# An mLSTM cell feeding a SwiGLU block: the first group's own results in two halves of 64 tokens, and a new order of the prologue

## The chip, the cores and the metric

The kernel runs on one core of a Trainium2 chip. The metric is the device time in microseconds, the median over several executions. One more execution is taken by the hardware profiler. The engines are TensorE (PE; PEld is its weight load), VectorE (DVE), ScalarE (ACT), GpSimd (POOL) and SyncE (SP), which only issues transfers.

## The reference

Two parts follow one another. The first is an mLSTM cell over 4 batches of 8 heads, 768 tokens and head size 40, a recurrence with stabilised gates:

```
m_new  = max(f + m, i);  f_stab = exp(f + m - m_new);  i_stab = exp(i - m_new)
C      = f_stab * C + i_stab * outer(v, k);   n = f_stab * n + i_stab * k
y      = sigmoid(o) * (C @ q) / max(|n . q|, 1)
```

The result, 3072 tokens of 320 features, goes through a SwiGLU block with 1536 hidden features: `(silu(x @ w_gate) * (x @ w_val)) @ w_out`. The weights come as 64-bit floating-point numbers, so that the kernel has to convert them; everything else is float32.

## The kernel before, in words

**Tiling.** The 768 tokens of each of the 4 batches are cut into 6 groups of 128 tokens. A group of all four batches has 512 rows, which is the width of a matmul in the SwiGLU block. While TensorE does the SwiGLU block of one group (12 hidden blocks of 128 features, `hidden`, L643, then the projection), the cell of the next group is computed in between. Nothing can run ahead of the first group's cell, so the kernel has a prologue of its own for it, and that is what the change rewrites.

**The prologue.** The recurrence is computed in parallel form within the group: weights of decay between every pair of tokens (`W0`, exponentials of gate sums, zero where the key comes after the query), multiplied by the scores q.k (`first_scores`, L513), multiplied by the values (`first_own`, L527). The values carry a column of ones, so that the product also gives the denominator. A unit `u` is one batch, that is 8 heads; a half `P` is two batches. `first_turn` (L503) transposes keys and queries by TensorE, `first_x` (L532) divides by the denominator, `first_gate` (L541) multiplies by the sigmoid of the output gates (`sig`, L462), `first_seam` (L558) transposes the result into the layout that the SwiGLU block reads, and `first_state` (L547) makes the state that the next group starts from, which `first_kept` (L555) copies out of PSUM. `first_values` (L499) prepares the values for that state on GpSimd. `burn` (L466) is dummy matmuls that keep TensorE from standing idle.

**The weights.** A piece of the 64-bit weights is asked for by `piece_load` (L140): the gate half goes into partitions 0 to 63 on SP's queue and the value half into partitions 64 to 127 on ScalarE's queue. A block of it is converted in three steps: `scale` (L185; ScalarE scales the upper and then the lower 32-bit words), `join` (L195; two VectorE operations shift and mask the upper part) and `rounded` (L204; an integer addition of the lower part, on VectorE where the call says V, else on GpSimd). The first hidden block needs block 0, the second block 1, and so on. Pieces 2 and 3 land in memory that the hidden results will use later; piece 2's is also part of `W0`, so that it is asked for only when the third own product has been made.

**Order.** There is no scheduler: each engine and each queue runs its instructions in the order of the program's calls and waits only on semaphores. An instruction that waits holds up all that stands behind it on its engine, the transfers that the engine issues among them. PSUM is given out in two rings of four banks, "cell" and "gen". `late_sums` (L273; a scan on VectorE, then a clearing and a subtraction on GpSimd) belongs to the gates of the later groups and is needed by `late_maxima`, which runs behind the first hidden block.

Of the kernel before, what the change touches and what calls it, by code (L numbers as in the profile page):

```python
# [19 lines left out]
SUB = 64  # L20
# [4 lines left out]
def kernel(  # L25
# [50 lines left out]
    def bank(name, tag="cell"):  # L76
        return psum.tile([128, 512], F32, name=name, tag=tag)
# [41 lines left out]
    def copy(eng, dst, src):  # L119
        if eng is nc.scalar:  # L120
            nc.scalar.copy(dst, src)
        else:
            eng.tensor_copy(dst, src)
# [58 lines left out]
                for c in range(0, n, 2):  # L182
                    blocks[NFC + (m + c) // 2] = (lo[:, c:c + 2], hi[:, c:c + 2], wo_sb[:, m + c:m + c + 2, :])

    def scale(j):  # L185
        if j in blocks:
            lo, hi, dst = blocks[j]
            a, d = hi.shape[1], hi.shape[2]
            top = conv.tile([128, NKC * 128], F32, name="top", bufs=1).rearrange("p (a d) -> p a d", a=a)
            nc.scalar.mul(top, hi.bitcast(F32), 2.0 ** -112)  # L190
            low = conv.tile([128, NKC * 128], I32, name="low").rearrange("p (a d) -> p a d", a=a)
            nc.scalar.mul(low, lo, 2.0 ** -29)
            blocks[j] = (low, top.bitcast(U32), dst)

    def join(j):  # L195
        if j in blocks:
# [76 lines left out]
    def late_sums():  # L273
        nc.vector.tensor_tensor_scan(flat(f_sb), flat(keep1), flat(f_sb), 0.0, op0=ALU.mult, op1=ALU.add)
        nc.gpsimd.memset(step1, 0.0)
        nc.gpsimd.tensor_sub(i_sb, i_sb, f_sb)
# [11 lines left out]
    M_dram = tc.dram_tile([BH, S - L], F32, name="M_dram")  # L288


    def turn_one(P, src, dst, engs):
        tp = [bank("tp_kq").rearrange("p (a t) -> p a t", t=SUB) for _ in range(2)]
        for a in range(UA):
            h = P * UH + 2 * a
            for i in range(2):
                nc.tensor.transpose(tp[i][:, a, :], src[half(i), h:h + 2, :].rearrange("p h d -> p (h d)"),  # L296
                                    ident[half(i), half(i)])
        for i in range(2):
            copy(engs[i], dst[:, P * UA:(P + 1) * UA, half(i)], tp[i])
# [128 lines left out]
    def xT(n):  # L428
        return xTs[max(n - 1, 0) % 2]
# [32 lines left out]
    def sig(P):  # L462
        nc.scalar.activation(o_sb[:, heads(P)], o_sb[:, heads(P)], AF.Sigmoid)
# [8 lines left out]
        return slice(u * BH, (u + 1) * BH)  # L472

    A, V, G = nc.scalar, nc.vector, nc.gpsimd
    HH = H // 2
    wps = {}

# [26 lines left out]
    def first_turn(P, src, dst, engs):  # L504
        for b in range(2):
            tp = bank("tp_kq").rearrange("p (a t) -> p a t", t=L)
            for a in range(UA // 2):
                h = P * UH + b * H + 2 * a
                nc.tensor.transpose(tp[:, a, :], src[:, h:h + 2, :].rearrange("p h d -> p (h d)"), ident)  # L509
            a = P * UA + b * UA // 2  # L510
            copy(engs[b], dst[:, a:a + UA // 2, :], tp)
# [15 lines left out]
    def first_own(u):  # L527
        first_y[u] = bank("first_y", "gen")[:, 0:H * D1].rearrange("p (h d) -> p h d", d=D1)
        for h in range(H):
            nc.tensor.matmul(first_y[u][:, h, :], lhsT=W0[:, u * H + h, :], rhs=v_sb[:, u * H + h, :], start=True, stop=True)  # L530

    def first_x(u):  # L532
        y = first_y.pop(u)
# [4 lines left out]
        nc.vector.tensor_tensor(x_sb[:, u, 0:DM].rearrange("p (h d) -> p h d", d=D), y[:, :, 0:D],  # L538
                                den.to_broadcast([128, H, D]), op=ALU.mult)

    def first_gate(P):  # L541
        for u in (2 * P, 2 * P + 1):
            x = x_sb[:, u, 0:DM].rearrange("p (h d) -> p h d", d=D)
            nc.vector.tensor_tensor(x, x, o_sb[:, u * H:(u + 1) * H], op=ALU.mult)
# [10 lines left out]
    def first_kept(P, ps, eng):  # L555
        copy(eng, state(2)[:, P * UA:(P + 1) * UA], ps)

    def first_seam(P, engs):  # L558
# [53 lines left out]
    nc.scalar.activation(warm, warm, AF.Silu)  # L612
    piece_load(4, wo_sb)
    piece_load(5)
# [106 lines left out]
        for P in range(2):  # L721
            load(dst, a, n, P)

    run = lambda f, *a, **b: (lambda: f(*a, **b))


    on_vector = (9, 10, 11)
# [125 lines left out]
```

## Time and profile before

| what | value |
|---|---|
| runs before | 552.24, 552.34, 552.70 us; median 552.34 |
| profiled execution | 551.99 us, its span 550.0 us |
| TensorE busy | 544.9 us (99%), granted clock 1.00 |
| VectorE, ScalarE, GpSimd busy | 236.1, 136.1, 103.0 us |
| first matmul of the SwiGLU block | 32.04 us from the start of the span |
| busy from 15.00 to 32.04 us | TensorE 16.69, VectorE 14.08, ScalarE 8.20, GpSimd 4.15 us |
| second output gates | asked for at 16.83 us, landed 8.2 us later |
| first weights, gate half | asked for at 19.43 us, landed 8.8 us later |

Times in the profile count from the start of the span. Busy time of an engine is the union of its instructions; matmuls are pipelined, so a busy TensorE is not one at its peak. A row of the timeline merges consecutive instructions of one line and gives the idle time ahead of them and what ended it. A float32 matmul leaves two records, [...]; a transpose leaves one. The chain that ended last is followed back from the last instruction to whatever released it.

### The profile page before, as it was taken

The page shows a single profiled execution, that of the slowest core. Times are in us where ns is not written, and L with a number is a line of the kernel's source. Part 1 is how long each engine was busy: PE and PEld are TensorE (multiplying, and loading weights), DVE is VectorE, ACT ScalarE, POOL GpSimd, SP SyncE. Part 2 cuts the span into 40 slices and gives each one's busy share as a digit, 9 for nine tenths or more (in the row PEclk, how much of TensorE's full clock was granted, in tenths as well). Part 3 has the DMA queues.
Part 4 walks back from the last instruction along what each step waited for, and adds up shares of the span by engine and source line. Part 5 has one row for each costly group of instructions (what it writes and reads, how often), then busy time and mean ns, then how long its engine had stood idle before and what let it go on. Part 6 is the DMA issues. An engine that isn't in the chain of part 4 may idle for free.

```text
span 550.0 us, 11592 instructions
## 1 busy us (share of the span) xinstructions
PE 544.9 (99%) x4989; PEld 311.4 (57%) x4989; DVE 236.1 (43%) x397; ACT 136.1 (25%) x203; POOL 103.0 (19%) x95
## 2 busy tenths in 40 slices
PE   8999999999999999999999999999999999999997
PEld 4964556774555575545575545576455567444475
DVE  5778668961346232455421545531436621111100
ACT  4376755352110133011024101115110100111100
POOL 2304265673011060011133011124001100000000
PEclk9999999999999999999999999999999999999999
DMA  9999997878431762660564551395000131000000
GB/s 123 177 294 184 188 277 154 146 104 118 53 49 23 120 112 64 74 74 11 87 117 104 63 72 14 59 146 113 1 1 2 32 63 40 12 1 0 2 24 24
DMA packets 223994, 45.69 MB, mean 83 GB/s; under 512 B 214504, under 2 KB 219112, under 8 KB 223944
## 3 DMA queue, kind: packets, MB, share of 16 engines
q1 hardware_dynamic: 222036, 42.11, 46.7%
q10 hardware_dynamic: 1908, 2.85, 1.9%
q8 instruction: 39, 0.64, 0.5%
q14 instruction: 11, 0.09, 0.1%
HBM read 35.68 MB, written 4.01 MB: 72 GB/s over the span
## 4 chain that ended last, share of the span: by engine, by line
PE 98%; DVE 1%; ACT 0%; issue 0%; ACTq 0%; DVEq 0%
PE gv_ps L651 57%; PE o_ps L667 24%; PE o_ps L674 5%; PE inter L377 2%; PE sp L331 2%; PE intra L382 2%; PE add L353 1%; PE first_y L530 1%; PE burn L469 1%; PE tp_kq L509 1%; PE sp L519 1%; PE wps L480 0%; PE tp_kq L296 0%; PE wps L484 0%; PE wps L489 0%; PE tp_x L439 0%
## 5 line engine op out<-in xcount | busy, mean ns | idle before, releaser
L651 PE MATMUL gv_ps<-xT,wgv_sb 64*128 64x512 f32 x1440 | 316.6, 593 | 0.3 <-DVE wgv_sb L207 0.3
L651 PEld LDWEIGHTS gv_ps<-xT,wgv_sb 64*128 64x128 f32 x1440 | 138.1, 187 | 159.1 <-issue 156.4
L657 DVE TENSOR_TENSOR h_sb<-sg,gv_ps 128x512 f32<-128x512 f32 x72 | 49.5, 688 | 212.3 <-ACT sg L656 212.3
L667 PE MATMUL o_ps<-wo_sb,h_sb 128*128 128x320 f32 x480 | 130.5, 433 | 0.0
L667 PEld LDWEIGHTS o_ps<-wo_sb,h_sb 128*128 128x128 f32 x480 | 90.8, 190 | 41.0 <-issue 3.8
L656 ACT ACTIVATE sg<-gv_ps 128x512 f32<-128x512 f32 x72 | 43.0, 597 | 263.7 <-PE gv_ps L651 263.7
L456 POOL TENSOR_SCALAR_AFFINE_SELECT w_sb<-w_sb 64x1024 f32<-64x1024 f32 x20 | 28.5, 1423 | 63.9 <-DVE w_sb L451 62.9
L362 POOL TENSOR_TENSOR C<-C,dec 128x328 f32<-128x328 f32 x20 | 14.5, 738 | 134.8 <-DVE C L369 134.8
L661 ACT COPY z_sb<-o_ps 128x320 f32<-128x320 f32 x24 | 10.0, 423 | 93.2 <-PE o_ps L667 89.4
L403 POOL TENSOR_TENSOR o_sb<-o_sb,y_sb 128x640 f32<-128x640 f32 x10 | 14.2, 1431 | 78.9 <-DVE y_sb L394 78.9
L674 PE MATMUL o_ps<-wo_sb,h_sb 128*128 128x320 f32 x96 | 26.9, 437 | 0.0
L451 DVE TENSOR_TENSOR w_sb<-g_T,w_sb 128x1024 f32<-128x1024 f32 x10 | 13.1, 1354 | 28.6 <-DMA w_sb<-M_dram 28.6
L426 DVE STREAM_TRANSPOSE xT<-x_sq 128x640 f32<-128x640 f32 x16 | 12.5, 822 | 22.9 <-DMA x_sq<-x_sb 22.9
L674 PEld LDWEIGHTS o_ps<-wo_sb,h_sb 128*128 128x128 f32 x96 | 17.9, 190 | 7.2
L394 DVE TENSOR_TENSOR y_sb<-y_sb,intra 64x328 f32<-64x328 f32 x40 | 19.7, 492 | 0.7
L369 DVE TENSOR_TENSOR C<-C,add 40x328 f32<-40x328 f32 (+1 forms) x36 | 17.7, 493 | 1.2 <-POOL C L362 0.6
L377 PEld LDWEIGHTS inter<-C,qT 64*64 64x64 f32 x640 | 10.2, 134 | 7.3 <-issue 6.1
L460 ACT ACTIVATE w_sb<-w_sb 128x1024 f32<-128x1024 f32 x10 | 10.6, 1058 | 12.7 <-POOL w_sb L456 12.7
L207 POOL TENSOR_TENSOR wgv_sb<-wgv_sb,low 128x640 int32<-128x640 int32 x6 | 9.3, 1546 | 23.5 <-DVE wgv_sb L200 23.5
L341 POOL TENSOR_TENSOR vw_sb<-v_sb,w_sb 128x656 f32<-128x656 f32 x10 | 12.8, 1306 | 0.4
L338 DVE TENSOR_TENSOR w_sb<-sp,w_sb 128x512 f32<-128x512 f32 x20 | 12.7, 682 | 0.0
L397 DVE TENSOR_SCALAR den<-den 128x16 f32<-128x16 f32 x10 | 12.2, 1215 | 0.3
(132 smaller groups left out, 344.5 us busy)
## 6 DMA issues: line engine op xcount, KB each, us to landing
w_sb<-M_dram SPq DMA_DIRECT2D x10, 512.0 KB, 7.3
x_sq<-x_sb SPq DMA_DIRECT2D x128, 40.0 KB, 2.0
k_sb<-in_k_dram SPq DMA_DIRECT2D x12, 320.0 KB, 6.0
v_sb<-in_v_dram SPq DMA_DIRECT2D x12, 320.0 KB, 5.6
o_sb<-in_o_gate_dram SPq DMA_DIRECT2D x12, 320.0 KB, 5.5
raw<-in_moe_w_out_dram SPq DMA_DIRECT2D x3, 1280.0 KB, 7.5
out_dram<-z_sb SPq DMA_DIRECT2D x24, 160.0 KB, 1.8
q_sb<-in_q_dram SPq DMA_DIRECT2D x32, 64.0 KB, 2.3
```

The costliest lines, as they stand in the source:

```text
L362: nc.gpsimd.tensor_tensor(state(s + 1)[:, a], state(s)[:, a], dec[:, s - 2, a].unsqueeze(2).to_broadcast([128, UA, D1]), op=ALU.mult)
L369: nc.vector.tensor_tensor(c, c, ps[r], op=ALU.add)
L377: nc.tensor.matmul(inter[two][half(i), a, :], lhsT=qT[half(two), P * UA + a, half(i)], rhs=state(2 * n + i)[half(two), P * UA + a, :], sta ...
L394: nc.vector.tensor_tensor(t, t, intra[i][half(c)], op=ALU.add)
L403: eng.tensor_tensor(o, o, y[:, :, 0:D], op=ALU.mult)
L451: nc.vector.tensor_tensor(w_sb[:, heads(P)], gb, w_sb[:, heads(P)], op=ALU.subtract)
L456: nc.gpsimd.affine_select(w, w, compare_op=ALU.is_ge, fill=NEG, base=0, pattern=[[0, UH], [1, SUB]], channel_multiplier=-1)
L651: nc.tensor.matmul(ps[i], lhsT=wgv_sb[half(i), m, PAIRS[kc][i] if g < 2 else kc, :], rhs=x[half(i), kc, :], start=(kc == 0), stop=(kc == N ...
L656: nc.scalar.activation(sg, ps[0], AF.Silu)
L657: nc.vector.tensor_tensor(hid(g, m), sg, ps[1], op=ALU.mult)
L667: nc.tensor.matmul(p, lhsT=hid(g, m)[:, ts(u, L)], rhs=wo_sb[:, m, :], start=(m == 0), stop=(m == NFC - 1))
L674: nc.tensor.matmul(ps[u], lhsT=hid(g, m)[:, ts(u, L)], rhs=wo_sb[:, m, :], start=(m == 0), stop=(m == NFC - 1))
```

## The change

Five things are changed, all ahead of the first hidden block or beside it.

1. The own product of a unit is made in two halves. Queries 64 to 127 take all 128 keys, queries 0 to 63 only the first 64 keys, and the two land in different partitions of one bank.
2. The keys and queries of the second half of the batches are transposed by `turn_one`, the form of the later groups, which works on 64 tokens at a time and takes two banks.
3. The order is new: the second own product comes between the transposes of the second half's keys and those of its queries, no longer behind both, the first state ahead of the first seam, and the calls of `burn` are others (7 more at the start in both; 6 before, 14 after).
4. The first piece of weights is asked for ahead of the second output gates, and the second piece directly behind them, ahead of the first `sig`. `scale` is split in two, so that the upper words of block 0 are scaled, and the block joined, ahead of the second `sig` and the second gating. The second gating, the second `sig` and the lower words come behind the first copy of the first seam. The first gating is made by GpSimd.
5. `late_sums` moves from behind the first own product to behind the conversion of block 1. Both state copies are ScalarE's.

```diff
-    def scale(j):
+    def scale_top(j):
...
+    def scale_low(j):
...
+    def scale(j):
+        scale_top(j)
+        scale_low(j)
...
-            nc.tensor.matmul(first_y[u][:, h, :], lhsT=W0[:, u * H + h, :], rhs=v_sb[:, u * H + h, :], start=True, stop=True)
+            n = u * H + h
+            nc.tensor.matmul(first_y[u][half(1), h, :], lhsT=W0[:, n, half(1)], rhs=v_sb[:, n, :], start=True, stop=True)
+            nc.tensor.matmul(first_y[u][half(0), h, :], lhsT=W0[half(0), n, half(0)], rhs=v_sb[half(0), n, :], start=True,
+                             stop=True)
...
-            nc.vector.tensor_tensor(x, x, o_sb[:, u * H:(u + 1) * H], op=ALU.mult)
+            eng.tensor_tensor(x, x, o_sb[:, u * H:(u + 1) * H], op=ALU.mult)
...
             copy(eng, xT(0)[:, c:c + len(cs), 2 * P * L:(2 * P + 2) * L].rearrange("p c (u s) -> p c u s", u=2), tp)
+            for f in between.get(c, ()):
+                f()
...
     first_own(0)
-    late_sums()
-    first_turn(1, k_sb, kT, (A, A))
+    turn_one(1, k_sb, kT, (A, A), "gen")
+    first_own(1)
+    turn_one(1, q_sb, qT, (A, V))
     first_x(0)
-    first_turn(1, q_sb, qT, (A, V))
+    piece_load(0)
     load(o_sb, o_gate, 0, 1)
-    piece_load(0)
-    first_own(1)
+    piece_load(1)
     first_values(1)
+    burn(3)
     first_scores(1)
     first_x(1)
     sig(0)
-    piece_load(1)
-    burn(3)
+    burn(2)
     first_own(2)
     piece_load(2, h_sb[:, 1:1 + NKC])
-    sig(1)
     burn(2)
     first_own(3)
-    first_gate(0)
+    ps0 = first_state(0, "gen")
+    burn(2)
+    first_gate(0, G)
     first_x(2)
     first_x(3)
-    first_gate(1)
-    first_seam(0, (A, A, V))
-    scale(0)
+    scale_top(0)
+    join(0)
+    first_seam(0, (A, A, V), {0: [run(sig, 1), run(first_gate, 1, V), run(scale_low, 0)]})
     ps1 = first_state(1, "gen")
-    burn(1, "gen")
+    burn(5)
     piece_load(3, h_sb[:, NH - NKC:])
-    join(0)
+    rounded(0, V)
     first_seam(1, (A, A, V))
-    rounded(0, V)
-    first_kept(0, first_state(0), A)
-    first_kept(1, ps1, V)
+    first_kept(0, ps0, A)
+    first_kept(1, ps1, A)
     convert(1, V)
+    late_sums()
     nc.scalar.activation(warm, warm, AF.Silu)
```

More of the change, by code (lines that the diff above doesn't have):

```diff
@@ L190, in scale @@
             nc.scalar.mul(top, hi.bitcast(F32), 2.0 ** -112)
+            blocks[j] = (lo, top.bitcast(U32), dst)
+    def scale_low(j):
+        if j in blocks:
+            lo, *rest = blocks[j]
+            a, d = lo.shape[1], lo.shape[2]
             low = conv.tile([128, NKC * 128], I32, name="low").rearrange("p (a d) -> p a d", a=a)
             nc.scalar.mul(low, lo, 2.0 ** -29)
-            blocks[j] = (low, top.bitcast(U32), dst)
+            blocks[j] = (low, *rest)
+    def scale(j):
+        scale_top(j)
+        scale_low(j)
     def join(j):
@@ L288, with turn_one @@
     M_dram = tc.dram_tile([BH, S - L], F32, name="M_dram")
-    def turn_one(P, src, dst, engs):
-        tp = [bank("tp_kq").rearrange("p (a t) -> p a t", t=SUB) for _ in range(2)]
+    def turn_one(P, src, dst, engs, tag="cell"):
+        tp = [bank("tp_kq", tag).rearrange("p (a t) -> p a t", t=SUB) for _ in range(2)]
         for a in range(UA):
@@ L474 @@
     A, V, G = nc.scalar, nc.vector, nc.gpsimd
+    run = lambda f, *a, **b: (lambda: f(*a, **b))
     HH = H // 2
@@ L539, in first_x, with first_gate @@
                                 den.to_broadcast([128, H, D]), op=ALU.mult)
-    def first_gate(P):
+    def first_gate(P, eng):
         for u in (2 * P, 2 * P + 1):
             x = x_sb[:, u, 0:DM].rearrange("p (h d) -> p h d", d=D)
-            nc.vector.tensor_tensor(x, x, o_sb[:, u * H:(u + 1) * H], op=ALU.mult)
+            eng.tensor_tensor(x, x, o_sb[:, u * H:(u + 1) * H], op=ALU.mult)
         nc.gpsimd.tensor_copy(x_sb[:, 2 * P:2 * P + 2, DM:], x_sb[:, 2 * P:2 * P + 2, 0:HP])
@@ L556, in first_kept, with first_seam @@
         copy(eng, state(2)[:, P * UA:(P + 1) * UA], ps)
-    def first_seam(P, engs):
+    def first_seam(P, engs, between={}):
         for c, eng in zip(range(0, NKC, 2), engs):
@@ L722, in load_all @@
             load(dst, a, n, P)
-    run = lambda f, *a, **b: (lambda: f(*a, **b))
     on_vector = (9, 10, 11)
```

## The prediction

> **What bounds it now.** I read the engines' busy shares first: TensorE is busy 544.9 of 550.0 us. The waits of TensorE then name the only places where it stands still after its first 1.2 us, 0.7 us in all.
>
> ```profile
> PE gv_ps L651 <- DVE wgv_sb L207: 0.3, 1, 0.3
> PE sp L519 <- ACT qT L121: 0.2, 1, 0.2
> PE first_y L530 <- DVE h_sb L523: 0.2, 1, 0.2
> ```
>
> So everything after the first gate/value matmul (32.04 us) is TensorE without a gap. The change touches only what lies before it and the three blocks after it: its worth is the shift of that start, call it G, plus any stall that it makes behind G. The chain that ended last shows what sets G (start, length, what):
>
> ```profile
> 25.39 1.73 PE first_y L530 x16
> 27.78 0.49 DVE x_sb L538
> 28.27 0.80 DVE x_sb L544 x2
> 29.43 0.50 DVE wgv_sb L199
> 29.95 0.83 DVE wgv_sb L200
> 31.08 0.83 DVE wgv_sb L207
> 32.04 17.51 PE gv_ps L651 x80
> ```
>
> TensorE's last own product releases DVE, and DVE goes through dividing, gating and joining the first weights. The timeline of TensorE shows that it was itself busy until 31.76 us, so G has two bounds 0.3 us apart: a gain must shorten both. Rows with the prices I need (start, length, engine, line, shapes, count):
>
> ```profile
> 18.63 1.88 PE L530 MATMUL first_y<-v_sb,h_sb 128*128 128x41 f32 x16
> 28.15 1.13 PE L552 MATMUL add<-vw_sb,k_sb 128*64 128x41 f32 x32
> 17.73 1.06 PE L509 MATMUL tp_kq<-ident,q_sb 128*128 128x128 f32 x8
> 59.57 0.66 PE L296 MATMUL tp_kq<-ident,k_sb 64*128 64x64 f32 x16
> 25.72 0.74 ACT L463 ACTIVATE o_sb<-o_sb 128x640 f32<-128x640 f32 x1 [3.61 <-DMA raw<-in_moe_w_val_dram]
> 16.10 1.47 DVE L274 TENSOR_TENSOR_SCAN f_sb<-keep,f_sb 32x640 f32<-32x640 f32 x1
> 58.53 1.14 DVE L199 TENSOR_SCALAR wgv_sb<-top 128x640 uint32<-128x640 uint32 x1 [0.91 <-ACT top L190]
> 57.77 1.55 POOL L207 TENSOR_TENSOR wgv_sb<-wgv_sb,low 128x640 int32<-128x640 int32 x1 [2.55 <-DVE wgv_sb L200]
> ```
>
> [...] the shift at 58.53 takes 1.14 us under GpSimd's addition, which ends at 59.32, and 0.49 us elsewhere. [...] the first 128*64 product's weights load at 28.151, 0.20 us after the last transpose began, where 0.11 is normal; after a 41-column product a change takes 0.155 us instead of 0.05 or less. No run here alternates two shapes on disjoint parts of the array. [...] for the small weights: 198 GB/s at 26 to 30 us.
>
> **The change, part by part.**
> TensorE. An own product of 16 records (1.71 us start to next) becomes 16 products in two column halves. The 128*64 rows of the state (32 records, pairs 0.058 us apart) give 16 x 0.058 = 0.93 us if the halves run side by side: -0.8 us, four times, -3.2. The second half's transposes become 16 small ones, 0.5 us for 1.07, twice: -1.1. Dummy matmuls grow from 6 to 14 at 0.22: +1.8. On the path to the second seam transposes: own(0) ends at 15.9, k turned 16.45, own(1) 17.5, q turned 18.0, dummies 18.7, wait for DVE's copy until 19.0, scores to 21.15, dummies and the wait for the second weighing 21.8, own(2) and dummies 23.35, own(3) 24.4, first state 25.35, dummies 25.85, first seam 27.05, second state 28.0, five dummies 29.15. Before, the same transposes began at 29.45 with a state (1.13) still behind them; now nothing is: TensorE is free for G at 30.35.
>
> DVE. It loses the scan ahead of dividing (1.47) and one gating pair (2 x 0.44, now GpSimd's, about 0.72 each by half of its 1.43 us row of 640; they end at 24.9, a microsecond before TensorE asks). Weighing of the second half starts at 20.5 instead of 21.7, the last division ends at 26.1, and the join (0.50 + 0.83) waits for the weights' upper half from ScalarE, not for the gates. It can be over by 28.0.
>
> Transfers. On SP's queue the first weights' gate half goes ahead of the second output gates (o1); on ScalarE's queue both value halves are issued at about 18.3 and 19.0, ahead of the first sigmoid and no longer behind its wait for the output gates. In the record of landings, o1 came at 24.99, then the second value half 26.54 and the first gate half 28.27. In the new order these two are ahead of o1. If transfers go one after the other, o1 lands 28.27 - 24.99 = 3.3 us later, at 28.3. Gate and value halves go to different partitions: from 33 to 40 us, with both queues at work, the rate was 351 GB/s, and two of 0.33 MB would take 1.9 us: o1 at 26.9. I take 27.6. From there: sigmoid 0.74 with its start-up, DVE's gating pair 0.9, four transposes and their drain 0.75, ScalarE's copy 0.55, handovers 0.35: G = landing + 3.3 = 30.9. The other bounds are below it: TensorE's 30.35 plus its first chunk's copy gives 30.6; rounding (0.82), after gates 29.3 and a copy 0.43, ends at 30.6. G moves by -1.15 us (-0.4 with the late landing, -1.45 if TensorE binds).
>
> Behind G. ScalarE's two state copies (0.43 each) now stand between the seam copies and the second block's upper half. That starts at G + 1.25, not G + 0.1, so the second join and rounding end at G + 4.35 instead of 35.28 - 32.04 = G + 3.24; the block is asked for at G + 4.37. With the handover: +0.1. Then comes the moved scan (1.47): DVE is free at G + 5.85 for the first product of the hidden block, which before began at G + 5.19. Behind the scan GpSimd sets a tile to zero (0.62) and subtracts (1.53, the row at 18.22): about G + 5.9 to G + 8.1. [...] The remaining 0.35 + 0.83 + 0.95 put the block at G + 10.25; before it was ready at 40.28, G + 8.24, and asked for at G + 8.76. Stall: about 1.5 us. [...] The fourth block is rounded by GpSimd behind DVE's second scan; it had 0.23 us to spare (ready 44.93, asked 45.16) and loses it: +0.2. Nothing later had under 1 us.
>
> Sum: -1.15 + 0.1 + 1.5 + 0.2 = +0.65 us. The profiled execution took 551.99 us (span 550.0 and 2.0 around it), so 552.65; the median of the runs, 552.34, is 0.35 above it: 553.0.
>
> **Rivals.**
> 1. Faster: [...] the subtraction gets in ahead of DVE's join or the second block comes earlier. For it: by this working DVE idles 1.7 us ahead of the second join, in which an earlier landing or shorter copies would pull everything forward. Against it: the order on DVE is fixed, scan before join. With no stalls and TensorE binding, 552.34 - 1.15 to 1.45 = 550.9 to 551.2. It decides if the scan ends before about G + 4.3.
> 2. The second output gates come late. Their 2,048 pieces of 160 B are still being served when ScalarE's queue asks for the next value half (0.66 MB, 3.3 us at 198 GB/s; now issued near 23.2, before 25.04). For it: before, o1's tail ran down from 274 to 7 packets a quarter microsecond as the value half came in. Against: o1 is asked for three microseconds before it. Landing 30 to 31.5, G = 33.3 to 34.8, and with 1.8 behind: +3.1 to +4.6, 555.4 to 557.
> 3. Alternating 128-row and 64-row products [...]. Two changes per head at 0.155 and two steps of 0.07: 0.45 a head, 3.6 us a product instead of 0.93; four changes give 5. TensorE then sets G: 4 x 2.7 more, less what hid in waits, G near 41: 561 and up. For it: the gaps above [...]. Against: the halves share no part of the array, [...]. A milder form, no gain at all from the split (1.8 us each), has G near 34: 556. It decides for slower once a product costs more than about 1.1 us.
>
> **How the numbers follow.** A measurement of this kernel tells from no change what is over 0.2%, 1.1 us: under 551.2 is faster, over 553.4 slower. My forecast has 0.44; its own range is 552.3 to 553.9, of which I count 0.33 as same and 0.11 as slower (a landing after 28). Rival 1 has 0.25, rival 2 0.13, rival 3 0.18, of which 0.06 the mild form. Faster 0.25, same 0.33, slower 0.42. The range 550.8 to 557 [...].
>
> **What would show it.** Own products at 0.93 us with pairs of records 0.06 apart (over 1.1: rival 3). First hidden matmul at 30.6 to 31.6, released by a seam copy, with o1's sigmoid ended near 28.4 (after 30: rival 2). TensorE waiting some 1.5 us for DVE's rounding at the third block, and a DVE shift of over 1.5 us under GpSimd's subtraction at about G + 6.5 (none: rival 1). Wrong would be a wait that I have not named, the first weights landing after 27, or a clock under 1.00 where TensorE waits.

## The result, and the profile after

The changed kernel takes 572.95 us (median of four, 572.12 to 573.18) against 552.52 us for the kernel before (552.24 to 552.77): a ratio of 1.0367, 95% interval 1.0349 to 1.0385. It is slower by 20 us. The profiled execution's span is 569.7 us, 19.7 more than the 550.0 before.

The waits of TensorE in the changed kernel (line waited for, then total, times and longest in us) tell nearly nothing of these 19.7 us:

```profile
PE gv_ps L668 <- DVE wgv_sb L217: 0.8, 1, 0.8
PE inter L387 <- issue: 0.5, 1, 0.5
...
PE tp_x L578 <- issue: 0.2, 1, 0.2
```

TensorE is never long without work; it is the work that takes longer. Its timeline (start, length, engine, line, rows*columns of the array, shapes, count) shows where. First the start of an own product at full speed, then one later, then the end of the stage:

```profile
14.91 0.31 PE L542 MATMUL first_y<-v_sb,h_sb 128*64 128x41 f32 x2
15.15 0.31 PE L543 MATMUL first_y<-v_sb,h_sb 64*64 64x41 f32 x2
15.39 0.31 PE L542 MATMUL first_y<-v_sb,h_sb 128*64 128x41 f32 x2
...
19.40 0.43 PE L542 MATMUL first_y<-v_sb,h_sb 128*64 128x41 f32 x2
19.76 0.43 PE L543 MATMUL first_y<-v_sb,h_sb 64*64 64x41 f32 x2
20.13 0.43 PE L542 MATMUL first_y<-v_sb,h_sb 128*64 128x41 f32 x2
...
40.47 1.93 PE L566 MATMUL add<-vw_sb,k_sb 128*64 128x41 f32 x32
43.16 2.33 PE L578 MATMUL tp_x<-ident,x_sb 128*128 128x128 f32 x10 [0.22 <-issue]
45.42 1.13 PE L566 MATMUL add<-vw_sb,k_sb 128*64 128x41 f32 x32
46.49 1.25 PE L479 MATMUL burn<-junk 128*128 128x512 bf16 x5
47.80 1.31 PE L578 MATMUL tp_x<-ident,x_sb 128*128 128x128 f32 x10
49.13 8.85 PE L668 MATMUL gv_ps<-xT,wgv_sb 64*128 64x512 f32 x40
58.77 1.56 PE L668 MATMUL gv_ps<-xT,wgv_sb 64*128 64x512 f32 x6 [0.78 <-DVE wgv_sb L217]
```

The two halves of a head never run side by side. Each half starts 0.237 us after the other, sixteen times a product: 3.79 us, where a product took 1.70 to 1.81 before (from its start to the start of what follows) and 0.93 was forecast. From 19.40 the same step takes 0.363 us, a product 5.8. A state takes 1.93 us at 40.47 and 1.13 at 45.42, ten transposes 2.33 and 1.31. That is a clock, and the busy times by stretch show it (PE, PEld, DVE, ACT, POOL busy us, then the granted clock of TensorE, DMA share, GB/s):

```profile
14.00:17.00 3.00, 2.96 (x30) 2.25 (x26) 2.05 (x4) 0.22 (x1) 0.27 (x2) 1.00 1.49 143
18.00:28.00 10.00, 9.78 (x72) 7.32 (x73) 1.50 (x5) 1.90 (x4) 1.29 (x1) 0.50 0.81 133
29.00:35.00 6.00, 5.85 (x55) 4.26 (x54) 3.95 (x11) 0.88 (x3) 2.01 (x3) 1.00 0.38 69
36.00:45.00 9.00, 8.78 (x68) 7.43 (x69) 2.25 (x6) 0.74 (x2) 0.00 (x0) 0.50 1.02 204
46.00:56.00 10.00, 9.92 (x67) 5.12 (x65) 6.74 (x12) 7.27 (x13) 1.58 (x3) 1.00 1.06 205
```

The record of the granted clock has two halved stretches, 18.05 to 28.29 and 35.11 to 45.35 us. TensorE counts as busy for 9.78 of 10 us in the first, and for all 3.00 us from 14 to 17, ahead of it: busy by the profile, and slowed all the same. In the kernel before the clock was 1.00 from 5.0 us to the end.

So the first hidden matmul (G in the prediction) starts at 49.13 instead of 32.04 us: 17.1 of the 19.7 us. Against the kernel before, the matmuls of the first two hidden blocks are 17.1 us late, those of the third 18.2 (it starts at 58.77 instead of 40.70) and those of the fourth 18.5 (63.48 instead of 44.99): 1.4 us more. The last 1.3 gathers in three steps of 0.3 to 0.5 us between 115 and 161 us. The stall at the third block looks as forecast, in the timelines of DVE and GpSimd:

```profile
53.19 1.47 DVE L284 TENSOR_TENSOR_SCAN f_sb<-keep,f_sb 32x640 f32<-32x640 f32 x1
54.59 0.65 DVE L674 TENSOR_TENSOR h_sb<-sg,gv_ps 128x512 f32<-128x512 f32 x1
55.16 0.52 DVE L209 TENSOR_SCALAR wgv_sb<-top 128x640 uint32<-128x640 uint32 x1
55.72 2.03 DVE L210 SCALAR_TENSOR_TENSOR wgv_sb<-top,wgv_sb 128x640 uint32<-128x640 uint32 x1
...
55.31 1.76 POOL L286 TENSOR_TENSOR i_sb<-i_sb,f_sb 32x640 f32<-32x640 f32 x1
```

The moved scan is followed by GpSimd's subtraction, and DVE's second join step takes 2.03 us under it instead of 0.83. The fourth block waits for an addition by GpSimd, which starts when DVE has joined that block. Its row in the kernel before, then in the changed one:

```profile
43.38 1.55 POOL L207 TENSOR_TENSOR wgv_sb<-wgv_sb,low 128x640 int32<-128x640 int32 x1 [13.95 <-DVE wgv_sb L200]
...
61.87 1.55 POOL L217 TENSOR_TENSOR wgv_sb<-wgv_sb,low 128x640 int32<-128x640 int32 x1 [4.80 <-DVE wgv_sb L210]
```

It ends 0.06 us ahead of the block in both (44.93 and 63.42). Before, TensorE reached the block at that moment anyway; in the changed kernel it was ready 0.3 us sooner and waited.

### The profile page after: what moved, and what is told of

Its sections match the earlier page's. It is cut to its first block, busy times and chain, and to the rows that moved or that the text cites. A ratio compares the mean times of both kernels' runs of the same rounds, so it can differ in the third digit from the quotient of the medians.

```text
span 569.7 us, 11767 instructions
## 1 busy us (share of the span) xinstructions
PE 562.9 (99%) x5074; PEld 321.1 (56%) x5077; DVE 236.2 (41%) x394; ACT 136.2 (24%) x204; POOL 104.9 (18%) x97
## 4 chain that ended last, share of the span: by engine, by line
PE 88%; DVE 1%; POOL 0%; issue 0%; ACT 0%; ACTq 0%; POOLq 0%
PE gv_ps L668 53%; PE o_ps L684 23%; PE o_ps L691 5%; PE inter L387 2%; PE sp L341 2%; PE intra L392 2%; PE add L363 1%; PE tp_kq L306 0%; POOL wgv_sb L217 0%; DVE M_sb L291 0%; PE tp_x L449 0%; DVE wgv_sb L210 0%; PE tp_g L642 0%; PE dec_ps L655 0%; ACT z_sb L678 0%
## 5 line engine op out<-in xcount | busy, mean ns | idle before, releaser
L691 PE MATMUL o_ps<-wo_sb,h_sb 128*128 128x320 f32 x96 | 26.9, 437 | 0.0
L404 DVE TENSOR_TENSOR y_sb<-y_sb,intra 64x328 f32<-64x328 f32 x40 | 19.7, 492 | 0.7
L190 ACT ACTIVATE top<-raw 128x640 f32<-128x640 f32 x12 | 9.6, 798 | 14.0 <-issue 5.5
```

The lines of the kernel that those rows point to most:

```text
L404: nc.vector.tensor_tensor(t, t, intra[i][half(c)], op=ALU.add)
L691: nc.tensor.matmul(ps[u], lhsT=hid(g, m)[:, ts(u, L)], rhs=wo_sb[:, m, :], start=(m == 0), stop=(m == NFC - 1))
```

## The experiments

Two theories for the 17 us stood against each other at first. The shape-change theory: it is the alternation between products of two forms (the form is the rows times columns of the array that a product takes: 128*64 and 64*64 here), and nothing else of the change. Rivals: half-width products are slow as such (A), or the new order and the transfers set the start (B). A summary first; G is the start of the first hidden matmul in the profiled execution; the product is the second one of the stage, from its start to the start of what follows. There is one profile of each kernel, and the first own product itself began between 14.31 and 15.38 us in them, ahead of every edit, so differences of G under a microsecond prove little by themselves.

| kernel | median us | ratio to before, interval | product us | G us | clock of the profiled run |
|---|---|---|---|---|---|
| before | 552.0 to 552.5 | | 1.8 | 32.04 | 1.000 |
| changed | 572.95 | 1.0349 to 1.0385 | 5.8 | 49.13 | 0.982 |
| same_shape | 556.37 | 1.0057 to 1.0103 | 1.1 | 32.79 | 0.999 |
| whole | 557.97 | 1.0085 to 1.0115 | 3.4 | 36.64 | 0.994 |
| split_alone | 568.52 | 1.0270 to 1.0318 | 4.3 | 48.40 | 0.982 |
| by_shape | 557.65 | 1.0083 to 1.0116 | 2.1 | 34.89 | 1.000 |
| burn_between | 578.54 | 1.0461 to 1.0489 | 8.0 | 57.08 | 0.976 |
| burn_heavy | 579.83 | 1.0477 to 1.0513 | 8.1 | 58.21 | 1.000 |
| whole_burn | 556.84 | 1.0062 to 1.0090 | 1.8 | 35.44 | 1.000 |
| sums_back | 554.87 | 1.0036 to 1.0079 | 1.1 | 34.94 | 0.997 |
| second_later | 557.09 | 1.0073 to 1.0119 | 1.1 | 31.38 | 1.000 |
| both_back | 555.50 | 1.0035 to 1.0076 | 1.1 | 31.14 | 1.000 |
| before_same | 552.12 | 0.9996 to 1.0016 | 1.1 | 31.42 | 0.999 |
| before_sp | 553.73 | 1.0020 to 1.0037 | 1.1 | 30.79 | 1.000 |
| before_sp_burn | 552.63 | 1.0001 to 1.0018 | 1.1 | 31.82 | 1.000 |

### The alternation: same_shape, whole, split_alone, by_shape

same_shape gives the lower half all 128 keys:

```diff
-            nc.tensor.matmul(first_y[u][half(0), h, :], lhsT=W0[half(0), n, half(0)], rhs=v_sb[half(0), n, :], start=True,
-                             stop=True)
+            nc.tensor.matmul(first_y[u][half(0), h, :], lhsT=W0[:, n, half(0)], rhs=v_sb[:, n, :], start=True, stop=True)
```

> The changed kernel with one edit: queries 0 to 63 also take all 128 keys (those above 63 have weight zero), so both halves of an own product are 128-row, 64-column products and the form never alternates inside a product. Shape-change theory: the halves run side by side, an own product takes 0.93 us instead of 3.8 at full clock, TensorE's clock stays at 1.00, the first hidden matmul starts at 30.6 to 31.6 us, total 551.5 to 554. Rival A, half-width products are slow as such (twice as many instructions): 3.5 us a product or more, clock falls again, 568 or more. Rival B, the new order and the later value halves of the first weights set the start: products are short, but the first hidden matmul stays past 38 us, total over 559.

It took 556.37 us, 16.6 less than the changed kernel, although the lower half now takes twice as many rows. Its TensorE timeline:

```profile
17.52 0.25 PE L542 MATMUL first_y<-v_sb,h_sb 128*64 128x41 f32 x1
17.53 0.25 PE L543 MATMUL first_y<-v_sb,h_sb 128*64 128x41 f32 x1
17.60 0.23 PE L542 MATMUL first_y<-v_sb,h_sb 128*64 128x41 f32 x1
17.61 0.23 PE L543 MATMUL first_y<-v_sb,h_sb 128*64 128x41 f32 x1
...
31.25 1.54 PE L577 MATMUL tp_x<-ident,x_sb 128*128 128x128 f32 x10 [0.99 <-DVE x_sb L557]
32.79 3.70 PE L667 MATMUL gv_ps<-xT,wgv_sb 64*128 64x512 f32 x16
```

Halves of one form start 0.01 us apart and the next pair 0.058 us later: sixteen steps make 0.93 us, as forecast for the change itself (1.06 to the start of what follows). Rivals A and B fall. But the total is 2.4 us above the expected range, and G 1.2 us: a rest of the change still costs 4.4 us, taken up below.

whole puts back the product of 128 rows and 128 columns:

```diff
-            n = u * H + h
-            nc.tensor.matmul(first_y[u][half(1), h, :], lhsT=W0[:, n, half(1)], rhs=v_sb[:, n, :], start=True, stop=True)
...
+            nc.tensor.matmul(first_y[u][:, h, :], lhsT=W0[:, u * H + h, :], rhs=v_sb[:, u * H + h, :], start=True, stop=True)
```

> The changed kernel with the own products whole again (128 rows, 128 columns, as in the kernel before), all else as changed. Shape-change theory: 1.75 us a product, clock 1.00, four times 0.82 more than with halves of one form, of which waits hide up to 1: first hidden matmul 32.5 to 34.5 us, total 553.5 to 557. Rival A (half width): the same as the theory here. Rival B (order and transfers): the first hidden matmul stays past 38 us, total over 559.

557.97 us: a microsecond over the range, and G at 36.64 instead of 32.5 to 34.5, because one expectation failed: the clock did not stay at 1.00. Its busy times by stretch:

```profile
17.70:24.40 6.70, 6.70 (x45) 5.39 (x46) 1.62 (x5) 2.37 (x4) 1.29 (x1) 0.50 1.06 180
24.50:34.00 9.50, 9.50 (x137) 8.58 (x135) 6.96 (x19) 3.43 (x6) 2.02 (x3) 1.00 0.91 177
```

Nothing alternates within a product here, and the clock is halved for 6.8 us. The fall of the clock is thus not tied to the alternation alone.

split_alone is the kernel before with only the changed `first_own`:

```diff
-            nc.tensor.matmul(first_y[u][:, h, :], lhsT=W0[:, u * H + h, :], rhs=v_sb[:, u * H + h, :], start=True, stop=True)
+            n = u * H + h
+            nc.tensor.matmul(first_y[u][half(1), h, :], lhsT=W0[:, n, half(1)], rhs=v_sb[:, n, :], start=True, stop=True)
+            nc.tensor.matmul(first_y[u][half(0), h, :], lhsT=W0[half(0), n, half(0)], rhs=v_sb[half(0), n, :], start=True,
+                             stop=True)
```

> The kernel before with one edit: each own product in the two halves of the changed kernel (128 rows for queries 64 to 127, 64 rows for queries 0 to 63, alternating by head); old order, old waits, old dummy matmuls. Shape-change theory: 3.8 us a product at full clock, four times 2.05 more than the whole product, total 560.5 if the clock holds; with the clock at half in two or three stretches, as in the changed kernel, 564 to 571. Rival B (order and transfers make the loss): 556 or less.

568.52 us, within the range for a clock that falls: the split by itself makes 16 of the 20 us, in the old order. The products began at 14.38, 21.66, 31.08 and 36.06 us and took 4.2, 4.3, 4.0 and 5.8 us to the start of what follows; three stretches at half clock, 20.5 us in all, as long together as in the changed kernel.

by_shape sorts the products of the changed kernel, so that a product changes form twice instead of sixteen times:

```diff
             nc.tensor.matmul(first_y[u][half(1), h, :], lhsT=W0[:, n, half(1)], rhs=v_sb[:, n, :], start=True, stop=True)
+        for h in range(H):
+            n = u * H + h
             nc.tensor.matmul(first_y[u][half(0), h, :], lhsT=W0[half(0), n, half(0)], rhs=v_sb[half(0), n, :], start=True,
                              stop=True)
```

> The changed kernel with the products of an own product sorted: first the eight of 128 rows, then the eight of 64 rows, two changes of form a product instead of sixteen. Shape-change theory: 16 records 0.055 us apart, a change, 16 more: 1.8 to 2.1 us a product, clock 1.00 or one short stretch below, total 554 to 558. If each 64-column product is dear whatever its neighbour (rival A): 3.5 us or more a product and 568 or more.

Its second product, and the transposes behind it:

```profile
17.49 1.13 PE L542 MATMUL first_y<-v_sb,h_sb 128*64 128x41 f32 x16
18.55 1.12 PE L545 MATMUL first_y<-v_sb,h_sb 64*64 64x41 f32 x16
19.60 0.71 PE L306 MATMUL tp_kq<-ident,q_sb 64*128 64x64 f32 x16
```

557.65 us and 2.1 us a product after the first, as expected: the same thirty-two records, and little over half the price (2.1 us for 3.79). Neither the half width nor the 64-row form is dear (sixteen records of either take 1.13 and 1.12 us); the change between the forms is.

### What halves the clock: burn_between, burn_heavy, whole_burn

In an alternating product the array streams 41 columns four times per head. A dummy streams 512 columns in about 0.22 us (five and a change from 46.49 to 47.80 us), so 41 columns take some 0.018 us and the array streams 15% of the 0.474 us of a head, by this estimate. The occupancy theory says that this small share, not the alternation as such, lowers the clock. burn_between puts one dummy behind every second head:

```diff
+            if h % 2:
+                nc.tensor.matmul(t, lhsT=junk[:, 0:128], rhs=junk, start=True, stop=True)
```

> The changed kernel with one dummy matmul (512 columns, 0.22 us at full clock) put behind every second head of each own product, sixteen in all: nothing is taken away, work is added. Clock theory (the alternating products leave the array so little occupied that the clock is halved for 10.2 us twice): the dummies keep it at 1.00 or shorten the slow stretches; a product takes 5 to 5.5 us at full clock against 3.8 and 5.8 before, transposes, scores and states run at full speed, the first hidden matmul starts at 45.5 to 48.5 us, sooner than the 49.13 of the changed kernel, total 569 to 572. If the clock falls for another cause (the order, the waits), the dummies only add: 4 to 6 us a product more or less as long as before plus 1.3, start at 53 us or more, total 576 or more.

It came out against the theory: 578.54 us, and two halved stretches of 13.65 us each, longer than without dummies.

```profile
20.00:33.00 13.00, 13.00 (x84) 8.55 (x85) 1.62 (x5) 2.97 (x5) 0.52 (x1) 0.50 0.53 97
34.00:39.00 5.00, 5.00 (x40) 3.15 (x37) 2.97 (x8) 0.00 (x0) 1.79 (x3) 1.00 0.21 35
```

By the same estimate, though, its array streams (0.14 + 0.22) / 1.27 = 28% of the time, still little. burn_heavy puts two dummies behind every head, which makes it 50%:

```diff
+            for _ in range(2):
+                nc.tensor.matmul(t, lhsT=junk[:, 0:128], rhs=junk, start=True, stop=True)
```

> The changed kernel with two dummy matmuls behind every head of each own product, 64 in all, four times the dose of burn_between: at full clock a product takes 7.5 to 8.5 us, of which the dummies stream 3.5. Occupancy theory: the clock now stays at 0.998 or more (the dose of burn_between, 17% of the time, was too small), transposes and scores run at full speed, first hidden matmul at 54 to 58 us although 10 us of work came to that of burn_between (57.1). If alternating products lower the clock whatever stands between them: mean clock 0.975 or less, first hidden matmul at 68 us or more, total over 588.

The clock stayed at 1.00 in all four executions, with every product still alternating:

```profile
14.00:24.00 10.00, 9.85 (x78) 5.30 (x76) 2.17 (x4) 1.04 (x3) 1.49 (x2) 1.00 1.21 166
24.00:34.00 10.00, 9.65 (x79) 5.34 (x81) 1.62 (x5) 1.54 (x3) 0.00 (x0) 1.00 0.13 20
```

48 dummies more than burn_between moved G by only 1.1 us. G came out at 58.21, just over what was expected; a head with its dummies takes 1.012 us. This kernel also splits the loss. The dummies add 1.012 - 0.474 = 0.538 us a head, 17.2 us for 32 heads; without them, at full clock, G would be about 41.0, by this estimate. From same_shape's 32.79 to 41.0 is the alternation at full clock, 8.2 us; from 41.0 to 49.13 the halved clock, 8.1 us.

whole_burn gives the kernel whole two dummies behind each of the first two own products:

```diff
     first_own(0)
+    burn(2)
     turn_one(1, k_sb, kT, (A, A), "gen")
     first_own(1)
+    burn(2)
```

> The kernel whole with four dummy matmuls more, two directly behind each of the first two own products (0.9 us of work at full clock). In whole every execution had a mean clock of 0.993 to 0.997, the profiled one 6.8 us at half clock from 17.6 us, although nothing alternates there. Occupancy theory (the clock is halved after some microseconds in which the array streams little; a whole own product streams 41 columns for each load of 0.11 us): the dummies keep the clock at 0.999 or more, the slow stretch goes, the first hidden matmul moves from 36.6 to 33.5 to 35.0 us, total 555.2 to 556.8 against 557.97. If occupancy is not the cause, or two dummies are too few: clock 0.993 to 0.997 as before, total 558 to 559.

556.84 us and G at 35.44, both just over the expectation, with the clock at 1.00 in all six executions where whole had 0.993 to 0.997 in all five. Adding 0.9 us of work moved G from 36.64 to 35.44. So in two kernels, one that alternates and one that doesn't, dummies brought the full clock back. In these runs the fall goes with how little the array streams: with alternation, by estimate, 15% and 28% of a head's time where the clock fell (changed kernel, burn_between) and 50% where it held (burn_heavy).

The traces of all fifteen kernels allow a count. The changes of the clock on record lie on a grid of 3.41 us (in the changed kernel halved stretches of 10.24 us with 6.83 us between them); cut by it, the stretches from 8 to 62 us can be compared by the share of time that the array streams (columns times 0.216 us for 512, the step between two dummies: an estimate). Nine times the clock falls. In the stretch ahead of the fall, ended 0.1 us before it, the array streamed 6 to 29% of the time (14 and 18.5% in the changed kernel); in the 207 others at full clock, 32% or more. The lowest of the kernel before has 32%, and whole's has 27%: this may be how the same whole products kept the clock in one order and lost it in another. No exact threshold is shown: the 0.1 us was chosen to fit (without it one of the nine has 35%), and at the very end of two kernels stretches with 20 and 23% kept the clock.

### The rest of the change: sums_back, second_later, both_back

same_shape is free of the alternation and still 4.4 us slower than before. Its profile has three places: G 0.75 us later, the third and fourth blocks 1.4 and 0.3 us further behind, and 1.6 us after 96 us. ScalarE, DVE and GpSimd at the first two:

```profile
29.85 0.74 ACT L473 ACTIVATE o_sb<-o_sb 128x640 f32<-128x640 f32 x1 [1.86 <-DMA o_sb<-in_o_gate_dram]
...
39.16 1.68 DVE L209 TENSOR_SCALAR wgv_sb<-top 128x640 uint32<-128x640 uint32 x1 [0.27 <-ACT top L190]
...
38.96 1.53 POOL L286 TENSOR_TENSOR i_sb<-i_sb,f_sb 32x640 f32<-32x640 f32 x1
```

The second output gates land at 29.82, and G follows by 2.97 us; the shift takes 1.68 us under the subtraction and ends 0.35 us behind it (40.84 and 40.49). sums_back moves `late_sums` back behind the first own product:

```diff
     first_own(0)
+    late_sums()
     turn_one(1, k_sb, kT, (A, A), "gen")
...
     convert(1, V)
-    late_sums()
```

> The kernel same_shape with late_sums back behind the first own product (its place in the kernel before), all else as it is there. [...] (the scan and GpSimd's subtraction hold up DVE's work for the third block): in same_shape the third block came 1.6 us later against the start of the first block than in the kernel before; that goes, since DVE idles 2.3 us at 17 us where the scan now stands, so total 554.6 to 555.5 against 556.37. Rival: the third block is late because everything ahead of it on ScalarE and DVE is late (two state copies, the later weights), and the scan only moves its wait: the third block still comes over 1 us late and the total stays within 0.5 us of 556.37, or the scan holds up the first division and the start comes later.

554.87 us: 1.5 less, and nothing is added at the third or fourth block (the shift is 2.90 at the start, 3.28 one pair of matmuls later and at both blocks). The first of the two expectations holds in the main: the edit moves scan and subtraction together, and the shift that took 1.68 us under the subtraction, instead of 0.49, is 1.2 of the third block's 1.4 us. The executions lie between 553.61 and 557.29. The profiled one, at 557.19, was one of the two slowest, and its trace shows what it met: the second output gates landed at 31.08, TensorE waited 3.2 us for them, and the clock was halved for 3.4 us from 32.28.

second_later asks for the second piece of weights behind the first `sig` (same_shape's order had it directly behind the second output gates):

```diff
-    piece_load(1)
     first_values(1)
...
     sig(0)
+    piece_load(1)
     burn(2)
```

> The kernel same_shape with the second piece of weights asked for behind the first sigmoid (its place in the kernel before), so that the second output gates stand ahead of it on both queues. Transfer theory (the start is the landing of the second output gates plus 3.0 us: 29.82 and 32.79 in same_shape): they land at 25.5 to 27.5, the first hidden matmul starts at 30.4 to 31.2, where TensorE's own work and the rounding of block 0 bind; total 554.2 to 555.2 if the third block's stall stays. Rival: the landing was not what bound, or the second piece is now late for the second block: start above 32 us or a new wait at the second block, total 556 or more.

Missed: the gates land at 28.25, G comes at 31.38, 1.4 us sooner than in same_shape, and the median is no better (557.09; the profiled execution, 554.75, is the fastest of six from 554.75 to 559.31). Three of the six have a mean clock of 0.994 to 0.997, and those took longest (557.43, 558.65, 559.31).

What lowers the clock in some executions of a kernel and not in others was not tested.

both_back makes the edits of sums_back and second_later together:

> Both edits, late_sums as in sums_back and the second piece as in second_later, on same_shape. If the two losses are separate and complete, they add: first hidden matmul 30.4 to 31.2 us, no stall at the third block, total 552.4 to 553.8 by same_shape's time and 550.8 to 551.5 by the start alone (32.04 before); the difference between the two is a delay of 1.4 us near 130 us in the profile of same_shape, where TensorE waits for ScalarE's output copies, which wait for output transfers, and of which I do not know whether it belongs to the change. If a third loss of the new order remains, 554 or more.

555.50 us (553.03 to 556.85): they do not add. G is at 31.14 and no stall of its own is left at the third block, but a new one stands at the second. The timelines of ScalarE and TensorE:

```profile
34.77 0.79 ACT L190 ACTIVATE top<-raw 128x640 f32<-128x640 f32 x1 [2.52 <-DMA raw<-in_moe_w_gate_dram]
...
37.96 2.42 PE L667 MATMUL gv_ps<-xT,wgv_sb 64*128 64x512 f32 x10 [2.26 <-DVE wgv_sb L217]
```

The gate half of the second piece lands at 34.61 instead of 29.99 in the kernel before. Its issue on SP's queue lasted from 20.16 to 24.25, while ScalarE's queue asked for the third piece at 23.01. The later request of second_later isn't what cost this: there the same half landed at 31.40, and in same_shape at 31.60, with the third piece asked for at 23.67 and 23.95. It was late in sums_back too (35.64, the third piece at 23.01), where the even later start hid it. So the loss came with `late_sums` in its old place and an earlier request of the third piece; which of them makes it was not tested.

### Is there a version that beats both: before_same, before_sp, before_sp_burn

before_same is the kernel before with the halves of same_shape:

```diff
-            nc.tensor.matmul(first_y[u][:, h, :], lhsT=W0[:, u * H + h, :], rhs=v_sb[:, u * H + h, :], start=True, stop=True)
+            n = u * H + h
+            nc.tensor.matmul(first_y[u][half(1), h, :], lhsT=W0[:, n, half(1)], rhs=v_sb[:, n, :], start=True, stop=True)
+            nc.tensor.matmul(first_y[u][half(0), h, :], lhsT=W0[:, n, half(0)], rhs=v_sb[:, n, :], start=True, stop=True)
```

> The kernel before with one edit: each own product in two halves of 64 columns, both over all 128 keys. Shape-change theory: 0.93 us a product instead of 1.75, clock 1.00. TensorE and DVE are done up to 3.2 us sooner, until the landing of the first weights' gate half (28.27 before) binds: join and rounding put the start at 30.7 to 31.3, total 550.9 to 551.6. Rival: splitting is worth nothing or costs, because the waits of the old order (weighing by DVE, second output gates) bind all along: 552 or more.

552.12 us against 552.32: no difference (interval 0.9996 to 1.0016), where 550.9 to 551.6 was expected, though G came 0.6 us sooner. That lead lasts to 96 us, and most of it is lost at one place (waits of TensorE):

```profile
PE inter L377 <- issue: 0.9, 1, 0.9
```

Behind the first 39 of 64 products of a later group TensorE stood still for 0.9 us with no wait that the profile shows. A gap of 0.3 to 1.0 us at this place is in the changed kernel, same_shape, split_alone, by_shape, sums_back, second_later, both_back and the two kernels below. The kernel before has a smaller one a little later, in the second half of the same stretch, so that what it costs against that kernel is less than the gap:

```profile
96.30 1.14 PE L377 MATMUL inter<-C,qT 64*64 64x41 f32 x64
97.26 1.56 PE L382 MATMUL intra<-v_sb,w_sb 64*64 64x41 f32 x64
```

From start to start these 128 products take 2.01 us in the later groups, here 2.44 in the kernel before and 3.18 in before_same, 2.50 to 3.25 in the others with a gap, 2.37 in whole_burn, and 2.01 to 2.13 in whole, burn_between and burn_heavy. The cause was not tested.

before_sp also asks for the second piece's value half on SP's queue:

```diff
-            queues = (nc.sync, nc.scalar if p < 5 else nc.sync)
+            queues = (nc.sync, nc.scalar if p < 5 and p != 1 else nc.sync)
```

> The kernel before_same (the kernel before with own products in two halves of 64 columns over 128 keys) and one edit more: the value half of the second piece of weights is asked for on SP's queue behind its gate half, no longer on ScalarE's. In before_same the chain of the first block starts at the landing of the first gate half (27.99), behind that value half (26.23). Transfer theory: it now lands 1.2 to 1.8 us sooner, the first hidden matmul starts at 29.9 to 30.6 instead of 31.4, total 550.3 to 551.2, against 552.1 for before_same and 552.3 for the kernel before. Rival: the landing of the gate half does not move (its own issue is late), or the second block's value half is now late for its turn: 551.5 or more.

The step worked in part: the first gate half lands at 27.13 instead of 27.99, 0.9 us sooner where 1.2 to 1.8 was expected, and G is 30.79. The total got worse, 553.73. The chain of waits behind G:

```profile
23.58 13.41 DMA h_sb<-in_moe_w_gate_dram
37.01 0.04 ACTq L190
37.05 0.05 issue
37.09 0.79 ACT top L190
37.88 0.02 issue
37.91 0.51 DVE wgv_sb L199
```

The third block waits for its own weights, which land at 36.99, and starts at 40.28, against 40.70 in the kernel before; the fourth waits for GpSimd again. A start 1.25 us sooner is worth 0.3 inside the third block and 0.07 from the fourth on. Then 0.8 is lost by 88 us and 0.5 in the gap named above.

before_sp_burn adds eight dummies to it, two with each own product:

```diff
     first_own(0)
+    burn(2)
...
     first_own(1)
+    burn(2)
...
-    burn(3)
+    burn(5)
     first_own(2)
...
-    burn(2)
+    burn(4)
     first_own(3)
```

> The kernel before_sp with eight dummy matmuls more, two with each own product: 1.8 us of work in place of the 3.2 us that the shorter products save on TensorE. Clock theory: executions of before_same with a clock below 0.998 took 553.8 to 555.2, those at 0.999 and 1.00 551.3 to 554.2; the dummies keep the clock at 1.00 in all executions and the times close together, median 550.3 to 551.3, no higher than before_sp. Rival: the clock is not at stake there, TensorE now binds and the start comes later by up to 0.8 us: 551.3 or more and above before_sp.

552.63 us, 1.1 below before_sp, above what was expected and not below the kernel before. The clock was 0.999 or 1.000 in all executions of both, so it isn't why. In the two profiled executions, which took the same time (553.34 and 553.35), G came at 31.82, 1.0 us later than in before_sp: a later start cost nothing there, because the start isn't what ends last. What the 1.1 us between the medians are is open. No version tried beats the kernel before.

## Why the prediction was wrong

**The step that failed** is the first one, "0.93 us if the halves run side by side". The forecast took the state's pairs as its row; those are two halves of one form. The argument against rival 3, "the halves share no part of the array", is what the runs refute: halves on disjoint columns but of 128 and 64 rows cost 3.79 us (changed kernel), halves of one form 0.93 (same_shape). A change of form costs time on disjoint columns too: 0.237 us a step with a change, 0.058 a pair without. What TensorE does in that time is not shown.

**Rival 3** had the right step, and its sizes were nearly right at full clock: 3.6 us a product forecast, 3.79 measured; G near 41 forecast, 41.0 by the estimate from burn_heavy. It was given 0.18, and at full clock the time would have been some 564 (41.0 - 32.04 = 9.0, and the 2.6 behind G, on 552.5). The other 8 us are the clock, which no rival had. The prediction looked for a low clock only "where TensorE waits". In the traces it does not wait there: TensorE was busy for 3.38 of the 3.42 us ahead of the first fall and for 9.78 of 10 us while slowed. All halved stretches that end ahead of the last matmul last 3.41, 6.83, 10.24 or 13.65 us, whole multiples of the first.

**The second half's transposes**, forecast at 0.5 us, took 0.64 (16.88 to 17.52 in same_shape). The rest of the path up to the gates was forecast well: in sums_back, where the stage began when it did before, weighing started at 20.50 and the last division ended at 26.09 (20.5 and 26.1 forecast).

**The landing of the second output gates**, forecast at 27.6 us (26.9 to 28.3): in the changed kernel they landed at 24.76, because ScalarE's value halves were not asked for at 18.3 but behind its copies of the late transposes:

```profile
19.50 1.07 ACT L121 COPY kT<-tp_kq 128x512 f32<-128x512 f32 x2 [5.28 <-PE tp_kq L306]
26.37 0.58 ACT L121 COPY qT<-tp_kq 128x512 f32<-128x512 f32 x1 [5.79 <-PE tp_kq L306]
26.37 1.35 ACTq L165 DMA_DIRECT2D raw<-in_moe_w_val_dram  x2
```

With the alternation gone, they were asked for at 19.34 and landed at 24.87 and 28.94, and the gates at 29.82: 2.2 us later than forecast, past the upper end that a strict queue gave. In sums_back they landed at 31.08, in second_later at 28.25 and in both_back at 28.17. This is rival 2's kind of loss by other transfers: in same_shape the last pieces of the gates (160 B each) share the time from 25 to 28 us with pieces of 1,024 B, of the first two pieces of weights; those of the third, 2,048 B, begin at 28. From there G = landing + 3.0 (3.3 forecast). So without the alternation G was 0.75 later in same_shape, not 1.15 sooner.

**The stalls behind G**, forecast as 0.1 at the second block, 1.5 at the third and 0.2 at the fourth, came as none, 1.1 and 0.3 us in the changed kernel and none, 1.4 and 0.3 in same_shape, and both are gone in sums_back. Right in place and cause, and near in size: 1.4 and 1.7 us for 1.8. The forecast had DVE's join of the third block go on only when GpSimd's subtraction is over, the author's estimate from the shift at 58.53 in the kernel before, which ended 0.35 us behind GpSimd's addition (59.67 and 59.32). In the changed kernel the second join step is the one held up (2.03 us for 0.83), the shift having got in ahead of GpSimd (0.52 us from 55.16, the subtraction from 55.31). The fourth block had less to spare than the forecast read: its first matmul stood at 44.99 in the kernel before, not at 45.16, 0.06 us behind the end of GpSimd's addition and not 0.23.

**What the sum left out** behind the first blocks: 1.3 us in the changed kernel, 1.6 in same_shape. Of these 0.3 and 0.5 are the gap in the later group. Another 0.5 and 0.6 come near 148 and 133 us, where TensorE's next weights wait 0.6 and 0.8 us (0.2 at this place before) for ScalarE's output copies, which wait for output transfers; the remaining 0.4 us shows by 161 and 146 us. Why these waits are longer after the change is open. In all, the change without the alternation is at 556.4 (same_shape), slower than the forecast of 553.0 as well, by a start mis-sized by 1.9 us and by these 1.6.

## What to carry to other kernels

Keep products that alternate on the array in one form: here a product whose lower half took 64 useless rows of zero weight was four times as fast as one without them (0.93 against 3.79 us at full clock). If two forms are needed, sort them (2.1 us). Where a stretch of several microseconds has many small products between loads, look at the granted clock and not only at the busy share (0.50 with TensorE busy for 9.78 of 10 us here); a few wide dummy matmuls can pay for themselves, as in whole_burn (G at 35.44 instead of 36.64), but too few can cost on both counts, as in burn_between (5.6 us slower than the changed kernel, clock 0.976 instead of 0.982). A gain at the start of a stage is only worth what the next transfer leaves of it (0.3 of 1.25 us inside the third block of before_sp): ask which block's weights land last before shortening what stands ahead.

## What the runs showed that was not expected

- A change of form between two 41-column products on disjoint columns costs 0.237 us from start to start at full clock and 0.363 at half clock.
- The clock can fall with TensorE busy nearly all the time (3.38 of the 3.42 us ahead of the changed kernel's first fall). By estimate it fell after 3.41 us with 6 to 29% of the time spent streaming, and held at 32% and more, from 8 to 62 us of the fifteen profiles.
- The second output gates (2,048 pieces of 160 B) landed 5.9 us behind their request where ScalarE's queue asked for nothing meanwhile (changed kernel), 10.2 us behind it where that queue asked for two weight halves within half a microsecond of it (same_shape), and 9.1 where the second of these came 1.5 us later (second_later).
- A gap of 0.3 to 1.0 us inside a group of small products, with no wait that the profile names, appeared in ten of the kernels; the kernel before has one of 0.3 us a little later in that group. Its cause is open.
